# Gate and up products of a gated MLP in the order 1, 7, 6, 2, 5, 3, 4, with their partial sums gathered in two PSUM banks

## The chip, the cores and the metric

The kernel runs on one core of a Trainium2 chip. The metric is the device time of one execution in microseconds (us). The engines are named as the profile names them: PE (TensorE, matrix products into PSUM), PEld (its weight loads), DVE (VectorE), ACT (ScalarE), POOL (GpSimd) and SP (SyncE, which here only issues DMAs). Each engine takes its instructions in the order in which the program lists them; an instruction whose semaphore is not there yet holds up all that stand behind it on the same engine.

## The reference

```python
def _A_ref(x, wqkv, wo):                      # linear attention, 32 heads of 18
    ...
    num = jnp.einsum("bhqd,bhde->bhqe", pq, kv)
    den = jnp.einsum("bhqd,bhd->bhq", pq, z)[..., None] + 1e-6
    o = num / den
    return ... @ wo

def _B_ref(x, w_gate, w_up, w_down):          # gated MLP, 576 -> 4608 -> 576
    g = jnp.einsum("bsd,df->bsf", x, w_gate)
    u = jnp.einsum("bsd,df->bsf", x, w_up)
    h = _gelu(g) * u
    return jnp.einsum("bsf,fd->bsd", h, w_down)

x = A_x                                        # 1 x 2048 x 576, float32
g = _sigmoid((x * gate_w).sum(-1, keepdims=True))
return g * _A_ref(x, ...) + (1 - g) * _B_ref(x, ...)
```

The change concerns the two products with `w_gate` and `w_up` in the second function.

## The kernel before, in words

The program has two parts. The first, some 300 us, projects keys, values and queries and forms the attention half, which goes to DRAM. The second is the MLP. It is a loop over n from 0 to 35 (lines 939 to 1033): 18 slices of 256 hidden columns for the first 1024 tokens (n below 18) and the same 18 slices for the second 1024 tokens. Each pass n has a **gate half** (m = 0) and an **up half** (m = 1).

In a half, the product of the inputs (two feature halves by two groups of 512 tokens) with the slice of weights (two feature halves by two groups of 128 columns) is a 2 by 2 block product. It is done with seven products instead of eight, from sums of the blocks of x (S1 to S4) and of the weights (T1 to T4); `PRODUCTS` (line 36) says which pair each of the seven numbers stands for. Float32 is kept by splitting every operand into a high and a low part, so one of the seven products is 7 matmuls of 512 columns into one PSUM bank (`product`, line 682). The four outputs are P1+P2; P1+P6+P7-P4; P1+P6+P5+P7; P1+P6+P5+P3. `gu_steps` (line 722) lists the seven steps of a half in the order 1, 6, 2, 7, 5, 4, 3. Each step issues one product and then the work of DVE and ACT that takes it out of its bank: step 1 copies P1 to `p1` with ACT (line 765), steps 6, 7, 5, 4 and 3 each add their bank to a running sum in SBUF on DVE (lines 770, 785, 790, 799, 816), and product 2 is added on top of product 1 in the same bank. Product 3 is added on top of product 5, once DVE has read product 5 there. In the gate half a GELU on ACT follows for each of the four outputs (`gelu`, and line 776 straight from PSUM); in the up half DVE multiplies the outputs with the gate (`up`, line 727), and `high` (ACT, line 730) and `low` (DVE, line 733) split the result `es` into `hs`. A half uses five of four rotating banks (`mlp.banks(4)`).

The down product of pass n-1 is spread between the steps of pass n by `next_down`. For n-1 below 18 and for the last pass it comes in 8 tiles of 12 matmuls (`down`, line 839). For n-1 from 18 to 34 (`BLOCKS`) it is a seven-product form too, 14 **units** of 6 matmuls (`unit`, line 870), each of which DVE adds into `sums` (line 881). Units and tiles use two PSUM pairs in turn. After a step i of the gate half two units follow from i = 2 on (in the last pass three from i = 3 on), and one tile from i = 3 on in the other passes; in the up half one follows each of the steps 0 to 3. Where n is 18 or 36, four (then all) tiles come first. So pass 0 has no down work between its steps, and the up halves of n = 18 and n = 35 have none either.

For the units, the rows of `h` must be summed as well: `h_sums` (line 743) has POOL add the four `es` in place, and in steps 0, 1 and 2 of the next pass (`late`) ACT takes the high parts and POOL the low parts (`h_parts`, line 739). The last of these high parts is the one of S4 (step 2), which waits for a sum on POOL that stands behind all the others there. The weights of the units are split by `d_split` (ACT line 678, POOL line 680) once the last unit of the pass before has read the old ones. In the first 18 passes POOL and ACT also split the gate and up weights (`w_sums`, `w_split`), which later passes load back from DRAM. In the last pass POOL combines the seven sums (`combine`, line 890), and DVE adds the attention half (`gated`, line 904).

## Time and profile before

| | us |
|---|---|
| runs | 1557.53, 1553.53, 1555.42; median 1555.42 |
| span of the profiled execution | 1554.6 |
| DVE busy | 989.5 |
| ACT busy | 548.6 |
| POOL busy | 851.2 |
| steps' copies out of PSUM, ACT L765, 72 of them | 43.0 |
| steps' first adds out of PSUM, DVE L770, 72 of them | 49.4 |
| one pass with units (from 1083.12 to 1116.92 on the chain) | 33.80 |

The span runs from the first to the last instruction of one execution. The profiled execution's own time outside its span is not given; its span stands 0.8 us below the median of the runs. A line such as `L690 PE MATMUL bank<-xo,wu` names the line of the program, the engine, the operation, the tile written and the tiles read; `x7` is how many instructions are merged in the row. In a timeline the first number is the start in us from the beginning of the span and the second the time until the end of the last merged instruction. Matmul ends include about 0.2 us of pipeline, so lengths of products are best taken from one start to the next.

### The profile page before, as it was taken

Reading aid. Unit: us, or ns where it says so; the run is one execution under the profiler, and the core shown is the slowest. Engines: PE = TensorE matmul, PEld = TensorE weight load, DVE = VectorE, ACT = ScalarE, POOL = GpSimd, SP = SyncE. Lnnn points to the kernel's source line nnn. Section 1 sums busy time; section 2 is a strip of 40 time slices with the busy share of each in tenths; the row PEclk is TensorE's granted clock in tenths of the full one; section 3 lists DMA queues with packets and bytes.
Section 4 is the critical chain, followed back from the end, with each engine's and each line's share of the span. In section 5 each row is a group of like instructions: output and inputs, shape, how many; then the busy total and the mean of one; then the engine's idle time right before and its main releaser. Section 6 shows DMA issues by size and latency. Waiting matters only on the chain.

```text
span 1554.6 us, 21238 instructions
## 1 busy us (share of the span) xinstructions
PE 1535.8 (99%) x8447; PEld 1358.3 (87%) x8447; DVE 989.5 (64%) x1342; ACT 548.6 (35%) x848; POOL 851.2 (55%) x693
## 2 busy tenths in 40 slices
PE   8999999999999999999999999999999999999997
PEld 8999788888888888888888888888888888888886
DVE  6443767366655555565655556777777767777777
ACT  6544554333433333333333322223232223222221
POOL 1410112276777768686666646556666555666663
PEclk9999999999999999999999999999999999999999
DMA  5611434765556565565545575433443443344333
GB/s 202 194 56 32 154 126 170 254 254 188 204 203 235 218 230 202 188 242 186 215 177 194 202 312 184 180 142 134 175 167 134 148 179 134 141 186 150 134 149 107
DMA packets 53883, 275.26 MB, mean 177 GB/s; under 512 B 4368, under 2 KB 23464, under 8 KB 43160
## 3 DMA queue, kind: packets, MB, share of 16 engines
q1 hardware_dynamic: 49464, 257.26, 44.5%
q10 hardware_dynamic: 2592, 9.31, 1.6%
q0 software_dynamic: 1728, 7.34, 1.2%
q8 instruction: 66, 1.08, 0.3%
q14 instruction: 33, 0.27, 0.1%
HBM read 172.41 MB, written 101.47 MB: 176 GB/s over the span
## 4 chain that ended last, share of the span: by engine, by line
PE 91%; DVE 4%; DMA 2%; issue 1%; ACT 1%; POOL 1%; SPq 0%; ACTq 0%; DVEq 0%; POOLq 0%
PE bank L690 50%; PE pair L852 15%; PE pair L876 12%; PE bank L168 7%; PE bank L333 3%; PE pair L524 2%; PE pair L219 1%; DVE h L733 1%; DMA xc<-xs 1%; DMA wg<-wp_d 1%; POOL xo L476 1%; DVE e L727 0%; DVE sums L904 0%; PE pair L168 0%; PE den L428 0%
## 5 line engine op out<-in xcount | busy, mean ns | idle before, releaser
L690 PE MATMUL bank<-xo,wu 128*128 128x512 f32 x1764 | 435.8, 394 | 5.7 <-DVE p L790 5.7
L690 PE MATMUL bank<-xo,wg 128*128 128x512 f32 x1764 | 433.7, 393 | 0.2 <-DMA wg<-wp_d 0.2
L690 PEld LDWEIGHTS bank<-xo,wu 128*128 128x128 f32 x1764 | 323.4, 188 | 66.7 <-DVE p L790 6.6
L690 PEld LDWEIGHTS bank<-xo,wg 128*128 128x128 f32 x1764 | 324.8, 188 | 64.7 <-DMA wg<-wp_d 0.6
L852 PEld LDWEIGHTS pair<-wd,h 128*128 128x128 f32 x1716 | 243.6, 189 | 13.8 <-DVE wd L67 0.7
L852 PE MATMUL pair<-wd,h 128*128 128x288 f32 x1716 | 250.6, 294 | 0.7 <-DVE wd L67 0.5
L730 ACT ACTIVATE h<-e 128x512 fp32r<-128x512 f32 x127 | 80.4, 633 | 376.3 <-DVE e L727 349.6
L859 DVE SCALAR_TENSOR_TENSOR acc<-pair,gate,acc 128x576 f32<-128x576 f32 x143 | 116.6, 816 | 131.1 <-PE pair L852 131.1
L881 DVE TENSOR_TENSOR sums<-pair,sums 128x576 f32<-128x576 f32 x224 | 167.7, 754 | 34.3 <-PE pair L876 26.5
L733 DVE TENSOR_TENSOR h<-e,h 128x512 fp32r<-128x512 f32 x127 | 131.4, 1035 | 44.8 <-ACT h L730 44.7
L760 ACT ACTIVATE e<-e 128x512 f32<-128x512 f32 x108 | 68.1, 631 | 226.1 <-DVE e L816 93.4
L680 POOL TENSOR_TENSOR wdb<-draw,wdb 128x432 fp32r<-128x432 f32 x34 | 38.4, 1153 | 195.9 <-ACT wdb L678 195.9
L876 PEld LDWEIGHTS pair<-wdb,h 128*128 128x128 f32 x816 | 117.9, 189 | 8.3 <-DVE sums L881 0.6
L876 PE MATMUL pair<-wdb,h 128*128 128x288 f32 x816 | 123.0, 296 | 0.1
L168 PE MATMUL bank<-kvw,xo 128*128 128x378 f32 (+5 forms) x560 | 106.9, 345 | 5.4 <-ACT kvw L66 5.2
L168 PEld LDWEIGHTS bank<-kvw,xo 128*128 128x128 f32 (+1 forms) x560 | 97.0, 192 | 9.9 <-ACT kvw L66 5.6
L618 POOL TENSOR_TENSOR wu<-wuraw,wu 128x768 fp32r<-128x768 f32 x18 | 36.5, 2028 | 119.6 <-ACT wu L617 119.6
L876 PEld LDWEIGHTS pair<-wdb,hx 128*128 128x128 f32 x612 | 89.0, 189 | 6.2 <-DVE sums L881 0.6
L876 PE MATMUL pair<-wdb,hx 128*128 128x288 f32 x612 | 93.0, 296 | 0.1
L765 ACT ACTIVATE p<-bank 128x512 f32<-128x512 f32 x72 | 43.0, 598 | 122.0 <-PE bank L690 121.6
L770 DVE TENSOR_TENSOR u<-bank,p 128x512 f32<-128x512 f32 x72 | 49.4, 686 | 45.0 <-PE bank L690 39.9
L727 DVE TENSOR_TENSOR e<-u,e 128x512 f32<-128x512 f32 x72 | 69.4, 965 | 2.5
(171 smaller groups left out, 2079.2 us busy)
## 6 DMA issues: line engine op xcount, KB each, us to landing
wp_d<-wg SPq DMA_DIRECT2D x17, 2240.0 KB, 6.7
wp_d<-wu SPq DMA_DIRECT2D x17, 2240.0 KB, 8.2
wg<-wp_d SPq DMA_DIRECT2D x17, 2240.0 KB, 8.7
wu<-wp_d SPq DMA_DIRECT2D x17, 2240.0 KB, 8.4
draw<-wdn SPq DMA_DIRECT2D x36, 576.0 KB, 9.4
wgraw<-wgu SPq DMA_DIRECT2D x18, 768.0 KB, 4.4
wuraw<-wgu SPq DMA_DIRECT2D x18, 768.0 KB, 4.5
xo<-xop_d SPq DMA_DIRECT2D x7, 1280.0 KB, 8.1
```

Of the source, the lines that this page charges most:

```text
L168: nc.tensor.matmul(out_t[:, :n], xa, kvw[i][:rows, r, lo:lo + n], start=(k == 0), stop=(k == 13))
L333: nc.tensor.matmul(ps[:R], qw[i][:rows, rw, GO[g]:GO[g] + R], xa, start=(k == 0), stop=(k == 13))
L690: nc.tensor.matmul(ps, w_, x_, start=start and i == 0, stop=i == 6, skip_group_check=not start)
L727: nc.vector.tensor_tensor(es[i], v, es[i], OP.mult)
L730: nc.scalar.activation(hs[i][:, 0], es[i], AF.Copy)
L733: nc.vector.tensor_tensor(hs[i][:, 1], es[i], f32(hs[i][:, 0]), OP.subtract)
L760: nc.scalar.activation(es[i], es[i], AF.Gelu_apprx_tanh)
L770: nc.vector.tensor_tensor(u2, b, p1, OP.add)
L852: nc.tensor.matmul(y[i], h[:, a, c], wd[:, (1 - i, 2 + i)[f], wl], start=(k == 0), stop=(k == 5))
L859: nc.vector.scalar_tensor_tensor(o, v, gate[:, 1, st:st + 1], o, op0=OP.mult, op1=OP.add)
L876: nc.tensor.matmul(y[:, j, :288], h[:, hl, c], wd[:, b, wl], start=(i == 0), stop=(i == 2))
L881: nc.vector.tensor_tensor(o, y[:, :, :288], o, OP.add)
```

## The change

The seven products of a half run in the order 1, 7, 6, 2, 5, 3, 4. Products 1, 6, 5 and 3 are added up in one bank; after 1, 6 and 5 ACT copies the sum so far to `p1`, `u2` and `u3` (`keep_copy`). Products 7 and 4 are added up in a second bank, from which DVE forms two outputs; for this, T4 has its sign turned (`b21 - t2`). Product 2 has a bank of its own, and DVE adds `p1` to it. Three of four banks are taken in a half. The down work of the up half follows steps 1 to 4 instead of 0 to 3, `d_prep` of a last pass moves from step 3 to 4, and `h_sums` and all its parts are queued behind the last step. The four banks of the MLP are opened before the first step instead of after the attention part is done.

```diff
-SEQUENCE = (1, 6, 2, 7, 5, 4, 3)
+SEQUENCE = (1, 7, 6, 2, 5, 3, 4)
...
+        def keep_copy(dst, src):
+            nc.scalar.activation(dst, src, AF.Copy)
         def s1():
             ps["a"] = bank()
             product(1, m, ps["a"], True)
-            nc.scalar.activation(p1, ps["a"], AF.Copy)
+            keep_copy(p1, ps["a"])
+        def s7():
+            ps["b"] = bank()
+            product(7, m, ps["b"], True)
         def s6():
-            b = bank()
-            product(6, m, b, True)
-            nc.vector.tensor_tensor(u2, b, p1, OP.add)
+            product(6, m, ps["a"], False)
+            keep_copy(u2, ps["a"])
         def s2():
-            a = ps["a"]
-            product(2, m, a, False)
+            c = bank()
+            product(2, m, c, True)
+            nc.vector.tensor_tensor(es[0] if m == 0 else p1, c, p1, OP.add)
             if m == 0:
-                nc.scalar.activation(es[0], a, AF.Gelu_apprx_tanh)
+                gelu(0)
             else:
-                up(0, a)
+                up(0, p1)
                 high(0)
                 low(0)
...
         def s5():
-            d = ps["d"] = bank()
-            product(5, m, d, True)
-            nc.vector.tensor_tensor(es[3] if m == 0 else p1, d, u3, OP.add)
+            product(5, m, ps["a"], False)
+            keep_copy(u3, ps["a"])
+            nc.vector.tensor_tensor(es[3] if m == 0 else u3, ps["b"], u3, OP.add)
             if m == 0:
                 gelu(3)
             else:
-                up(3, p1)
+                up(3, u3)
+        def s3():
+            product(3, m, ps["a"], False)
+            if m == 0:
+                nc.scalar.activation(es[1], ps["a"], AF.Gelu_apprx_tanh)
+            else:
+                up(1, ps["a"])
+                high(3)
+                low(3)
         def s4():
-            e = bank()
-            product(4, m, e, True)
-            nc.vector.tensor_tensor(es[2] if m == 0 else u3, u3, e, OP.subtract)
+            product(4, m, ps["b"], False)
+            nc.vector.tensor_tensor(es[2] if m == 0 else u2, ps["b"], u2, OP.add)
...
+                up(2, u2)
                 if blocks:
-                    late[1] = h_sums()
...
+                    then = h_sums()
+                    late[0] = lambda i: (i == 0 and (high(1), low(1)), then(i))
+                else:
+                    high(1)
+                    low(1)
+                    if seam:
+                        high(2)
+                        low(2)
+                    else:
+                        late[0] = lambda i: i == 0 and (high(2), low(2))
-        return [s1, s6, s2, s7, s5, s4, s3]
+        return [s1, s7, s6, s2, s5, s3, s4]
...
-            if i < 4:
+            if 0 < i < 5:
                 next_down()
-            if i == 3 and final:
+            if i == 4 and final:
                 d_prep(last)
             if blocks and i == 4:
                 d_split()
```

How the rows move, at three places. First ACT in a gate half with units (n from 19 to 35). `h`, `hx` are the parts of S3, S1, S2 and S4, `e` the four outputs, `p`, `u` the kept sums; what a row waits for stands in brackets. Before, from the first copy of the half to its last GELU:

```order
L765 ACTIVATE p1_2551<-bank_8551 128x512 [waits PE_49,Activation_49]
L730 ACTIVATE h0_2916<-e0_2554 128x512 [waits DVE_49]
L678 ACTIVATE wdb_8033<-draw2_8034 128x3x288 [waits DMAHW0_49,PE_49]
L678 ACTIVATE wdb_8033<-dsum_8035 128x4x288 [waits Pool_49]
L730 ACTIVATE h3_2919<-e3_2915 128x512 [waits DVE_49]
L765 ACTIVATE p1_2551<-bank_8665 128x512 [waits PE_49]
L730 ACTIVATE h1_2917<-e1_2913 128x512 [waits DVE_49,Activation_49]
L740 ACTIVATE hx1_8038<-sx_8036 128x512 [waits Activation_49,Pool_49]
L740 ACTIVATE h2_2918<-e2_2914 128x512 [waits Activation_49,Pool_49]
L740 ACTIVATE hx0_8037<-e3_2915 128x512 [waits Activation_49]
```

And now, from the same copy to the copy of `u3`:

```order
L731 ACTIVATE h0_2916<-e0_2554 128x512 [waits DVE_49]
L764 ACTIVATE u3_2553<-bank_8202 128x512 [waits PE_49,Activation_49]
L679 ACTIVATE wdb_7959<-draw2_7960 128x3x288 [waits DMAHW5_49,PE_49]
L679 ACTIVATE wdb_7959<-dsum_7961 128x4x288 [waits Pool_49]
L731 ACTIVATE h3_2919<-e3_2915 128x512 [waits DVE_49]
L764 ACTIVATE p1_2551<-bank_8314 128x512 [waits PE_49]
L731 ACTIVATE h1_2917<-e1_2913 128x512 [waits DVE_49]
L741 ACTIVATE hx1_7964<-sx_7962 128x512 [waits Pool_49]
L741 ACTIVATE h2_2918<-e2_2914 128x512 [waits Pool_49]
L741 ACTIVATE hx0_7963<-e3_2915 128x512
```

The row `hx_8039<-e` of before (now `hx_7965<-e`) is the high part of S4. Behind it stood GELUs of a finished output; now the copy of P1+P6+P5 to `u3` stands behind it and behind the first GELU.

Second, PE in the same gate half, from the fifth product on. `bank` rows are products, `pair` rows are units. Before, product 5, two units and product 4:

```order
L690 MATMUL bank_8745<-xo_130,wg_2445 128x512 x7
L876 MATMUL pair_8755<-wdb_8033,hx1_8038 128x288 [waits DVE_49,Activation_49]
L876 MATMUL pair_8755<-wdb_8033,hx1_8038 128x288
L876 MATMUL pair_8755<-wdb_8033,hx1_8038 128x288 [waits Pool_49]
L876 MATMUL pair_8755<-wdb_8033,hx1_8038 128x288 x3
L876 MATMUL pair_8763<-wdb_8033,hx1_8038 128x288 [waits DVE_49]
L876 MATMUL pair_8763<-wdb_8033,hx1_8038 128x288 x5
L690 MATMUL bank_8771<-xo_130,wg_2445 128x512 x7
```

Now product 5, two units and product 3:

```order
L691 MATMUL bank_8581<-xo_130,wg_2445 128x512 [waits Activation_49]
L691 MATMUL bank_8581<-xo_130,wg_2445 128x512 x6
L874 MATMUL pair_8671<-wdb_7959,hx1_7964 128x288 [waits DVE_49]
L874 MATMUL pair_8671<-wdb_7959,hx1_7964 128x288
L874 MATMUL pair_8671<-wdb_7959,hx1_7964 128x288 [waits Pool_49]
L874 MATMUL pair_8671<-wdb_7959,hx1_7964 128x288 x3
L874 MATMUL pair_8679<-wdb_7959,hx1_7964 128x288 [waits DVE_49]
L874 MATMUL pair_8679<-wdb_7959,hx1_7964 128x288 x5
L691 MATMUL bank_8581<-xo_130,wg_2445 128x512 [waits Activation_49]
L691 MATMUL bank_8581<-xo_130,wg_2445 128x512 x6
```

Before, neither product waited here. Now both are added to the same bank, and each waits for the ACT copy that reads it (of `u2` and `u3`).

Third, PE at the end of an up half, where the units are `pair` rows. Before, product 7, the last unit, and products 5, 4 and 3:

```order
L690 MATMUL bank_8608<-xo_130,wu_2446 128x512 x7
L876 MATMUL pair_8617<-wdb_8033,hx2_8039 128x288 [waits DVE_49]
L876 MATMUL pair_8617<-wdb_8033,hx2_8039 128x288 x5
L690 MATMUL bank_8625<-xo_130,wu_2446 128x512 x7
L690 MATMUL bank_8641<-xo_130,wu_2446 128x512 x7
L690 MATMUL bank_8625<-xo_130,wu_2446 128x512 [waits DVE_49]
L690 MATMUL bank_8625<-xo_130,wu_2446 128x512 x6
```

And now, from product 5:

```order
L691 MATMUL bank_8469<-xo_130,wu_2446 128x512 [waits Activation_49]
L691 MATMUL bank_8469<-xo_130,wu_2446 128x512 x6
L874 MATMUL pair_8545<-wdb_7959,hx2_7965 128x288 [waits DVE_49]
L874 MATMUL pair_8545<-wdb_7959,hx2_7965 128x288 x5
L691 MATMUL bank_8469<-xo_130,wu_2446 128x512 [waits Activation_49]
L691 MATMUL bank_8469<-xo_130,wu_2446 128x512 x6
L691 MATMUL bank_8479<-xo_130,wu_2446 128x512 [waits DVE_49]
L691 MATMUL bank_8479<-xo_130,wu_2446 128x512 x6
```

The last unit of the up half, which is the last that reads the old down weights, stood ahead of the last three products; now it stands ahead of the last two.

More of the change, by code (lines that the diff above doesn't have):

```diff
@@ L273, in make @@
             t1, t2, t3, t4 = (self.sums[:, i] for i in range(4))
-            for o, a, b in ((t1, b12, b11), (t2, b22, t1), (t3, b22, b12), (t4, t2, b21)):
+            for o, a, b in ((t1, b12, b11), (t2, b22, t1), (t3, b22, b12), (t4, b21, t2)):
                 nc.gpsimd.tensor_tensor(o, a, b, OP.subtract)
@@ L316, in tile_gated_mix @@
     mixing = Scope()
-    mixing.banks(3)
-    denp = mixing.stack.enter_context(tc.tile_pool(name="denp", bufs=1, space=PSUM, reuse_waits="tile"))
+    mixps = Scope()
+    mixps.banks(3)
+    denp = mixps.stack.enter_context(tc.tile_pool(name="denp", bufs=1, space=PSUM, reuse_waits="tile"))
     rp = mixing.pool("rp", bufs=3)
@@ L610, in w_sums @@
         t1, t2, t3, t4 = (tsum[:, i] for i in range(4))
-        for o, a, b in ((t1, b12, b11), (t2, b22, t1), (t3, b22, b12), (t4, t2, b21)):
+        for o, a, b in ((t1, b12, b11), (t2, b22, t1), (t3, b22, b12), (t4, b21, t2)):
             nc.gpsimd.tensor_tensor(o, a, b, OP.subtract)
@@ L764, in s1 @@
             product(1, m, ps["a"], True)
-            nc.scalar.activation(p1, ps["a"], AF.Copy)
+            keep_copy(p1, ps["a"])
+        def s7():
+            ps["b"] = bank()
+            product(7, m, ps["b"], True)
         def s6():
-            b = bank()
-            product(6, m, b, True)
-            nc.vector.tensor_tensor(u2, b, p1, OP.add)
+            product(6, m, ps["a"], False)
+            keep_copy(u2, ps["a"])
         def s2():
-            a = ps["a"]
-            product(2, m, a, False)
+            c = bank()
+            product(2, m, c, True)
+            nc.vector.tensor_tensor(es[0] if m == 0 else p1, c, p1, OP.add)
             if m == 0:
-                nc.scalar.activation(es[0], a, AF.Gelu_apprx_tanh)
+                gelu(0)
             else:
-                up(0, a)
+                up(0, p1)
                 high(0)
                 low(0)
-        def s7():
-            c = bank()
-            product(7, m, c, True)
-            nc.vector.tensor_tensor(u3, c, u2, OP.add)
         def s5():
-            d = ps["d"] = bank()
-            product(5, m, d, True)
-            nc.vector.tensor_tensor(es[3] if m == 0 else p1, d, u3, OP.add)
+            product(5, m, ps["a"], False)
+            keep_copy(u3, ps["a"])
+            nc.vector.tensor_tensor(es[3] if m == 0 else u3, ps["b"], u3, OP.add)
             if m == 0:
@@ L802, in s4 @@
             else:
-                up(2, u3)
-                high(3)
-                low(3)
+                up(2, u2)
                 if blocks:
-                    late[1] = h_sums()
-        def s3():
-            d = ps["d"]
-            if m == 1 and not blocks:
-                high(2)
-                if seam:
-                    low(2)
-            product(3, m, d, False)
-            nc.vector.tensor_tensor(es[1] if m == 0 else u2, d, u2, OP.add)
-            if m == 0:
-                gelu(1)
-            else:
-                up(1, u2)
-                if seam:
+                    then = h_sums()
+                    late[0] = lambda i: (i == 0 and (high(1), low(1)), then(i))
+                else:
                     high(1)
                     low(1)
-                elif blocks:
-                    late[0] = lambda i: i == 0 and (high(1), low(1))
-                else:
-                    late[0] = lambda i: i == 0 and (high(1), low(2), low(1))
-        return [s1, s6, s2, s7, s5, s4, s3]
+                    if seam:
[4 more added lines that the diff above has]
+        return [s1, s7, s6, s2, s5, s3, s4]
     def acc_load(p, t):
@@ L905, in gated @@
                                        mix_of(t).rearrange("p (n c) -> p n c", n=2), op0=OP.mult, op1=OP.add)
+    mixps.close()
+    mlp.banks(4)
     first_steps = gu_steps(0)
@@ L920, in tile_gated_mix @@
     mixing.close()
-    mlp.banks(4)
     hp0 = mlp.pool("hp0")
```

## The prediction

> **What bounds the kernel now.** I read the page's busy times first.
>
> ```profile
> span 1554.6 us, 21238 instructions
> ...
> PE 1535.8 (99%) x8447; PEld 1358.3 (87%) x8447; DVE 989.5 (64%) x1342; ACT 548.6 (35%) x848; POOL 851.2 (55%) x693
> ...
> L881 DVE TENSOR_TENSOR sums<-pair,sums 128x576 f32<-128x576 f32 x224 | 167.7, 754 | 34.3 <-PE pair L876 26.5
> ```
>
> PE is the bound: it is idle for 18.8 us in all. The change adds no matmul and takes none away, so it can win only from those 18.8 us, and it loses whatever new waits PE gets. The list of waits, PE alone, shows how little is to be won:
>
> ```profile
> PE bank L690 <- DVE p L790: 5.7, 2, 5.2
> ...
> PE bank L690 <- DMA wg<-wp_d: 0.2, 1, 0.2
> ```
>
> The first row is product 3 waiting for DVE to read product 5 out of the same bank: twice, once for 5.2 us (in the last pass). Between them stands nothing over 0.7 us in the MLP. So the question is whether the new waits for ACT are as well hidden as the old ones for DVE. I therefore took one pass with units from the timeline, engine by engine. PE, from the first product of a gate half (1087.78):
>
> ```profile
> 1087.78 5.00 PE L690 MATMUL bank<-xo,wg 128*128 128x512 f32 x21
> 1092.62 1.77 PE L876 MATMUL pair<-wdb,h 128*128 128x288 f32 x12
> 1094.23 1.79 PE L690 MATMUL bank<-xo,wg 128*128 128x512 f32 x7
> 1095.85 1.75 PE L876 MATMUL pair<-wdb,h 128*128 128x288 f32 x12
> ```
>
> Start to start, three products take 4.84 us (1.61 each), two units 1.60 (0.80 each). ACT and POOL in the same stretch:
>
> ```profile
> 1083.16 0.93 ACT L678 ACTIVATE wdb<-draw 128x864 fp32r<-128x864 f32 x1 [1.86 <-PE pair L876]
> ...
> 1089.60 0.60 ACT L765 ACTIVATE p<-bank 128x512 f32<-128x512 f32 x1 [2.01 <-PE bank L690]
> ...
> 1096.48 0.58 ACT L776 ACTIVATE e<-bank 128x512 f32<-128x512 f32 x1
> 1100.45 0.63 ACT L740 ACTIVATE hx<-e 128x512 fp32r<-128x512 f32 x1 [3.39 <-POOL e L737]
> 1100.98 0.62 ACT L760 ACTIVATE e<-e 128x512 f32<-128x512 f32 x1
> ```
>
> ```profile
> 1084.17 2.21 POOL L680 TENSOR_TENSOR wdb<-draw,wdb 128x432 fp32r<-128x432 f32 x2 [12.34 <-ACT wdb L678]
> 1086.33 3.73 POOL L680 TENSOR_TENSOR wdb<-dsum,wdb 128x576 fp32r<-128x576 f32 x2
> 1090.68 1.29 POOL L737 TENSOR_TENSOR e<-e,e 128x512 f32<-128x512 f32 x1 [0.63 <-DVE h L733]
> ...
> 1099.12 1.29 POOL L737 TENSOR_TENSOR e<-e,sx 128x512 f32<-128x512 f32 x1
> ```
>
> The reader is to see the row at 1100.45: ACT stands idle for 3.39 us until POOL's seventh instruction, counted from 1090.68, is through (1099.12 + 1.29 = 1100.41), and only then takes the high part of S4. Today this harms nobody: behind it is a GELU that PE does not wait for.
>
> **The change, part by part.**
>
> *The new wait in gate halves with units (n = 19 to 34, 16 passes).* In the ACT rows of the change, the copy to `u3` is third after this S4 part (S4, first GELU, `u3`), and product 3 cannot start before it. Without waits PE would run products 1, 7, 6 from 1087.78, two units from 1092.62, product 2 from 1094.22, two units, product 5 from 1097.43, two units from 1099.04 and product 3 from 1100.64. When is `u3` there? POOL's work is first moved later. The down weights are split once the last unit has read the old ones; that unit now stands one product (1.61) later, so ACT L678 starts at 1084.77, POOL's run over `wdb`, which ended at 1090.06, ends at 1091.67, and the sum that began at 1090.68 begins then, 0.99 later. From that sum to the S4 part on ACT the rows give 1100.45 - 1090.68 = 9.77, so S4 is taken at 1101.44. Back to back, ACT's starts lie 0.53 apart (1100.45 to 1100.98): GELU at 1101.97, `u3` at 1102.50, and with 0.60 for a copy out of a bank and 0.05 for the handover PE goes on at 1103.15. That is a wait of 1103.15 - 1100.64 = **2.5 us per pass**, 16 x 2.5 = 40.0. A part of it already falls on product 5, which waits for `u2` behind the parts of S3 and S1; the end is the same.
>
> Bounds for it: if S4 comes no later than today (1100.45), the wait is 1.5; if DVE never gets in POOL's way, the four splits take 2.21 + 2.75 (two of 576 columns, row at 1527.43 below) and end at 1090.74, and seven sums and parts of 1.29 end at 1099.8, which leaves 0.85. If DVE gets in the way once more (0.7, one of its instructions), 3.2. I take 2.5, the value with the contention that the rows show.
>
> *Pass 35, gate half.* Three units stand between products 5 and 3 and there are two pairs. The third unit needs the first one's pair, whose DVE add is queued behind the add that waits for `u3`: 1103.10 + 0.69 + 0.75 (L881's mean, 754 ns) and handovers make 1104.65. Its turn would be at 1087.78 + 4.84 + 1.60 + 1.61 + 2.40 + 1.61 + 1.60 = 1101.44. **3.2 us.** Queued behind the same add in the other passes are the sums of two units; the next unit wants its pair only after product 3, when they are done.
>
> *The other `u3` waits.* From the start of the next slot, ACT begins 0.20 after a product (1089.60 against 1087.78 + 1.61), copies 0.60 and hands over: 0.85. One unit (0.80) covers nearly all of it in up halves: 16 x 0.05 = 0.8. A tile or two units cover it in the other gate halves and in passes 1 to 17: 0. In pass 0 nothing covers it: 0.85 in its gate half. In the up halves of passes 0 and 18 nothing covers it either, and ACT first has the high part of the first output, which waits for two DVE instructions: from the end of product 2, 0.20 + 0.69 + 0.69 + 0.63 + 0.60 with handovers make 2.9, product 5 covers 1.61: 1.3 each. In pass 18 this hides the 0.2 that PE now waits for weights. Sum 0.8 + 0.85 + 1.3 + 1.1 = **4.0 us**.
>
> *The seam after pass 17.* The down product that follows at once uses outputs 3 and 2 first. Output 2 is now the last one made. The timeline of before:
>
> ```profile
> 914.25 1.88 PE L690 MATMUL bank<-xo,wu 128*128 128x512 f32 x7 [0.53 <-DVE p L790]
> ...
> 916.90 2.91 PE L852 MATMUL pair<-wd,h 128*128 128x288 f32 x20 [0.24 <-DVE h L733]
> ```
>
> These two waits (0.8) go. After the last product DVE still has a low part (until 1.0), then an add, the multiplication and two low parts of 0.7 each: 3.8. The first tile's last two matmuls (0.27) start then instead of ending with the tile at 1.6: 2.5 lost, 0.8 won: **+1.7**.
>
> *The last pass's up half.* Here is the old 5.2.
>
> ```profile
> 1507.98 19.48 POOL L890 TENSOR_TENSOR sums<-sums 128x576 f32<-128x576 f32 x14
> 1527.43 2.75 POOL L668 TENSOR_TENSOR wdb<-draw,wdb 128x576 fp32r<-128x576 f32 x2
> ```
>
> ```profile
> 1523.59 7.13 DVE L733 TENSOR_TENSOR h<-e,h 128x512 fp32r<-128x512 f32 x1 [0.70 <-ACT h L730]
> ...
> 1531.43 0.69 DVE L790 TENSOR_TENSOR p<-bank,u 128x512 f32<-128x512 f32 x1
> 1532.15 0.69 DVE L727 TENSOR_TENSOR e<-p,e 128x512 f32<-128x512 f32 x1
> ...
> 1532.17 3.35 PE L690 MATMUL bank<-xo,wu 128*128 128x512 f32 x7 [5.18 <-DVE p L790]
> 1532.76 0.81 DVE L904 SCALAR_TENSOR_TENSOR sums<-sums,gate,dsum 128x576 f32<-128x576 f32 x1
> ```
>
> A DVE instruction with both inputs in SBUF, 0.7 us elsewhere, took 7.13 because POOL's run of sixteen went through without a gap; all behind it were late. In the change, the first such instruction is the multiplication behind product 2, and the high part on ACT waits for it, `u3` behind that, product 3 behind that. Counted from the first product of this half (1517.16 before): POOL's fourteen end at 10.3 (the last two now come after, since the split they wait for moves behind product 5), multiplication to 11.05, high part, copy, product 3 at 12.3 instead of 8.05, product 4 to 15.5. DVE then still has ten instructions of 0.7 to 0.8 and one or two waits for ACT and POOL, and frees the first tile at about 20.9; two tiles end at 22.5. Before, they ended at 1539.34, which is 22.2. Term **+0.5**, between -3 (if DVE slips in earlier) and +5. The Trainium skill ("SBUF — State Buffer", section "Who interferes with whom") says that whichever of DVE and GpSimd issues first holds the shared port for that one instruction. By it DVE would wait 1.4 us at most and the term would be about 1.6 lower, the sum 1603. The row of 7.13 speaks against it here, so the trace's value stays.
>
> *What is removed.* Two of five DVE adds per half go (144 x 0.69 = 99 us), and two ACT copies come (144 x 0.60, less 36 GELUs that now read SBUF instead of a bank, at the same 0.6). PE waits for neither outside the places above, so both count nothing. Earlier banks before pass 0: the queries' banks are free by then, nothing.
>
> **Sum**: 40.0 + 3.2 + 4.0 + 1.7 + 0.5 = 49.4. On the span it gives 1604.0; the profiled span is 0.8 below the median of the runs, and 1555.4 + 49.4 = **1605**.
>
> **Rivals.**
> - *The S4 part comes in time* (not slower). ACT is busy a third of the time, and today PE never waits for a copy of it. Decided by S4's start: up to 1098.9 the wait is nothing (1100.64 less 1.71 for the rest of the chain). Then the small terms remain, 4.0 + 1.7 with +0.5 to -3 for the end: 1558 to 1562, the middle 1560; under 1551 only if the whole 5.2 at the end and the slow clock behind it were won and the small terms hidden too. Against it: POOL's row at 1099.12 alone ends after 1098.9, already before its shift.
> - *POOL runs freely*: waits of 0.85 and the small terms, 16 x 0.85 + 1.5 + 5 = 20, 1575. For it: DVE has 99 of its 989.5 us less to do. Against it: the instructions of DVE that collided with the splits remain.
> - *The clock falls in each wait.* After product 5 of the last pass PE stood still, and the granted clock (third column from the end of these windows) halved 3.4 us later:
>
> ```profile
> 1527.00:1530.30 3.30, 0.00 (x0) 0.00 (x0) 3.30 (x1) 0.00 (x0) 3.18 (x3) 1.00 0.69 216
> 1530.40:1537.00 6.60, 4.83 (x14) 4.15 (x15) 6.43 (x11) 1.26 (x2) 0.00 (x0) 0.50 0.00 1
> ```
>
> The half clock lasted 6.6 us, so each fall costs about 3.3: 17 x 3.3 = 56, 1661. It decides from a standstill of 3.4 us; mine is 2.5, in two pieces. The Trainium skill ("TensorE: Matmul & The Clock Gate", section "A second HAM failure mode: psum-queue depth-cycling") reports that even short, frequent idle times between bursts on cycling banks make the clock swing. By that page the time would be 1661; no row here shows it for gaps below a microsecond.
> - That the change doesn't do what it says is excluded by the rows: the copies stand there and PE waits for them.
>
> **Chances.** Forecast 0.74; POOL free 0.10; clock 0.06; S4 in time 0.10 (of it 0.03 faster, 0.06 the same, 0.01 slower). Low end: waits of 0.85 with the small terms and -3 at the end, 13.6 + 1.5 + 4.0 with 1.7 - 3, about +16 to 1571. High end: 16 x 3.2 + 4.2 + 5 + 2.5 + 5 = 68, 1624. Range 1570 to 1626; clock and "in time" are left out. A measurement of this kernel tells 0.3% (4.7 us) from no change: faster 0.03, same 0.06, slower 0.91.
>
> **What would show it.** In the list of waits, PE bank <- ACT `u` should lead with some 40 us in about 17 long and 17 or more short waits; a pass with units should take 36.3 instead of 33.8 us; ACT's S4 part should start 13.7 us after the first product of the gate half, and passes 1 to 17 should stay at their length. It is wrong if the S4 part comes before 11 us, if passes without units grow, or if the granted clock falls below 1 between 955 and 1500 us.

## The result, and the profile after

The changed kernel takes 1613.83 us (median of four runs, 1613.62 to 1614.31), the kernel before 1555.54 us in runs beside them (1553.53 to 1557.53): ratio 1.0372, 95% interval 1.0358 to 1.0387. It is slower by 58.3 us; the prediction had said 49.4.

The page of the changed kernel: span, busy times, and the groups of the products and of the new copies (busy us and mean ns, then the idle time ahead of the group and what ended it).

```profile
span 1612.2 us, 21093 instructions
...
PE 1552.9 (96%) x8447; PEld 1362.7 (85%) x8447; DVE 882.4 (55%) x1198; ACT 627.6 (39%) x992; POOL 854.0 (53%) x693
...
L691 PE MATMUL bank<-xo,wg 128*128 128x512 f32 x1764 | 439.3, 396 | 33.8 <-ACT u L764 33.7
L691 PE MATMUL bank<-xo,wu 128*128 128x512 f32 x1764 | 437.5, 395 | 5.0 <-ACT u L764 5.0
...
L764 ACT ACTIVATE u<-bank 128x512 f32<-128x512 f32 x144 | 85.0, 590 | 134.1 <-PE bank L691 134.1
```

And its list of PE's waits (us in total, times, longest):

```profile
PE bank L691 <- ACT u L764: 38.7, 41, 2.4
...
PE pair L874 <- DVE sums L879: 2.1, 1, 2.1
```

DVE has 107 us less to do than before, and the kernel is slower all the same: PE now idles for 59.3 us instead of 18.8, nearly all of the difference ahead of products that wait for a copy (L764) which takes ACT only 0.59. The reader is to see the releaser and the group together: a short instruction, with ACT busy 39% of the time, and 41 waits for it. It must have been late in starting, which the ACT rows below show. The span grew by 57.6 us, of which 40.5 are this idle time; the other 17.1 stand in PE's busy time (1552.9 against 1535.8). Modelled ends reach some 0.2 us into each wait, the products behind a wait take a little longer (see the end), and three stretches at half clock lengthen their matmuls.

Starts of the gate halves in the two traces give the length of each pass, and so where the time went. Up to the start of the last matmul the differences come to 57.7 us (the rest is rounding):

| stretch | before, us | after, us | difference | forecast |
|---|---|---|---|---|
| until pass 0 | 270.45 | 271.76 | +1.3 | 0 |
| pass 0 | 43.36 | 48.69 | +5.3 | +2.2 |
| pass 1 | 36.14 | 35.32 | -0.8 | 0 |
| passes 3, 5, ... 13, each | 35.33 | 36.02 to 36.09 | +4.3 in all | 0 |
| pass 17 (seam) | 42.99 | 44.63 | +1.6 | +1.7 |
| pass 18 | 29.45 | 30.91 | +1.5 | +1.1 |
| passes 20 to 34, each | 33.80 | 36.46 | +41.9 with pass 19 | +40.8 |
| pass 35 | 55.94 | 58.47 | +2.5 | +3.7 |

The first line is open: in the experiments that build on the changed kernel pass 0 starts between 270.7 and 272.0, in the one that builds on the kernel before (e4) at 269.8. The spread within one kind is as large as the difference, but the two kinds don't overlap, so a part of it may belong to the change. Pass 1 is shorter since the kernel before waits 0.5 there for down weights and the change, whose pass 0 is longer, does not.

Now one gate half with units, the same as in the prediction (pass 23), from the timeline of the changed kernel. PE:

```profile
1111.03 5.00 PE L691 MATMUL bank<-xo,wg 128*128 128x512 f32 x21
1115.87 1.77 PE L874 MATMUL pair<-wdb,h 128*128 128x288 f32 x12
1117.47 1.79 PE L691 MATMUL bank<-xo,wg 128*128 128x512 f32 x7
1119.10 1.75 PE L874 MATMUL pair<-wdb,h 128*128 128x288 f32 x12
1121.26 1.88 PE L691 MATMUL bank<-xo,wg 128*128 128x512 f32 x7 [0.41 <-ACT u L764]
1122.98 1.76 PE L874 MATMUL pair<-wdb,hx 128*128 128x288 f32 x12
1126.26 1.89 PE L691 MATMUL bank<-xo,wg 128*128 128x512 f32 x7 [1.51 <-ACT u L764]
```

ACT, and of POOL the beginning of its split of the down weights and the seventh of its instructions on `h`:

```profile
1107.03 0.60 ACT L764 ACTIVATE u<-bank 128x512 f32<-128x512 f32 x1 [0.31 <-PE bank L691]
1107.78 0.93 ACT L679 ACTIVATE wdb<-draw 128x864 fp32r<-128x864 f32 x1
...
1124.57 0.63 ACT L741 ACTIVATE hx<-e 128x512 fp32r<-128x512 f32 x1 [3.37 <-POOL e L738]
1125.11 0.61 ACT L761 ACTIVATE e<-e 128x512 f32<-128x512 f32 x1
1125.62 0.58 ACT L764 ACTIVATE u<-bank 128x512 f32<-128x512 f32 x1
```

```profile
1108.78 2.73 POOL L681 TENSOR_TENSOR wdb<-draw,wdb 128x432 fp32r<-128x432 f32 x2 [15.52 <-ACT wdb L679]
...
1123.25 1.28 POOL L738 TENSOR_TENSOR e<-e,sx 128x512 f32<-128x512 f32 x1
```

Without waits product 3 would start 12.87 after the first product. It starts at 1126.26, which is 15.23. Product 5 ended long before, near 1123. ACT stood idle for 3.37 us ahead of the row at 1124.57, the part of S4; only when POOL had made its sum (1123.25 + 1.28) did ACT go on to a GELU and then to the copy at 1125.62. The copy's own data had been there since product 5.

### The profile page after: what moved, and what is told of

It reads as the page before. It is cut to its first block, busy times and chain, and to the rows that moved or that the text cites. A ratio compares the mean times of both kernels' runs of the same rounds, so it can differ in the third digit from the quotient of the medians.

```text
span 1612.2 us, 21093 instructions
## 1 busy us (share of the span) xinstructions
PE 1552.9 (96%) x8447; PEld 1362.7 (85%) x8447; DVE 882.4 (55%) x1198; ACT 627.6 (39%) x992; POOL 854.0 (53%) x693
## 4 chain that ended last, share of the span: by engine, by line
PE 67%; POOL 15%; DVE 7%; ACT 6%; issue 4%; DMA 1%; SPq 0%; ACTq 0%; DVEq 0%; POOLq 0%
PE bank L691 34%; PE pair L850 12%; PE bank L168 7%; PE pair L874 7%; POOL wdb L681 5%; POOL e L738 4%; POOL hx L742 3%; PE bank L334 3%; PE pair L525 2%; DVE e L728 2%; POOL sx L738 1%; PE pair L219 1%; ACT wdb L679 1%; DVE h L734 1%; ACT wu L618 1%
## 5 line engine op out<-in xcount | busy, mean ns | idle before, releaser
L691 PE MATMUL bank<-xo,wg 128*128 128x512 f32 x1764 | 439.3, 396 | 33.8 <-ACT u L764 33.7
L681 POOL TENSOR_TENSOR wdb<-draw,wdb 128x432 fp32r<-128x432 f32 x34 | 46.3, 1383 | 249.0 <-ACT wdb L679 249.0
L734 DVE TENSOR_TENSOR h<-e,h 128x512 fp32r<-128x512 f32 x127 | 124.8, 983 | 36.0 <-ACT h L731 33.8
L764 ACT ACTIVATE u<-bank 128x512 f32<-128x512 f32 x144 | 85.0, 590 | 134.1 <-PE bank L691 134.1
L874 PEld LDWEIGHTS pair<-wdb,h 128*128 128x128 f32 x816 | 118.3, 189 | 9.6 <-DVE sums L879 2.6
L874 PE MATMUL pair<-wdb,h 128*128 128x288 f32 x816 | 123.3, 296 | 2.1 <-DVE sums L879 2.1
L764 ACT ACTIVATE p<-bank 128x512 f32<-128x512 f32 x72 | 43.2, 599 | 140.5 <-PE bank L691 140.1
L874 PEld LDWEIGHTS pair<-wdb,hx 128*128 128x128 f32 x612 | 89.5, 190 | 6.6 <-POOL hx L742 0.8
L874 PE MATMUL pair<-wdb,hx 128*128 128x288 f32 x612 | 93.3, 297 | 0.6 <-POOL hx L742 0.5
L793 DVE TENSOR_TENSOR e<-bank,u 128x512 f32<-128x512 f32 x36 | 24.9, 692 | 114.9 <-ACT u L764 114.9
```

The source lines that it names most:

```text
L681: nc.gpsimd.tensor_tensor(wd[:, i, 1, c], src[:, :, c], f32(wd[:, i, 0, c]), OP.subtract)
L691: nc.tensor.matmul(ps, w_, x_, start=start and i == 0, stop=i == 6, skip_group_check=not start)
L734: nc.vector.tensor_tensor(hs[i][:, 1], es[i], f32(hs[i][:, 0]), OP.subtract)
L764: nc.scalar.activation(dst, src, AF.Copy)
L874: nc.tensor.matmul(y[:, j, :288], h[:, hl, c], wd[:, b, wl], start=(i == 0), stop=(i == 2))
```

## The experiments

Ten kernels were run, each beside the kernel before on the same chip. Two theories stood against each other at first. **Queue**: the copies are late because ACT takes its instructions in order and stands at parts that wait for POOL. **Copy**: a copy out of a bank ahead of every further product is itself too long for the cover it has. The first experiments undo or move one thing each; the later ones take away, one by one, the waits that were left.

### e1: parts behind the copies

```diff
                 if i == 0:
                     h_parts(S2, sx)
-                elif i == 1:
+                elif i == 2:
                     h_parts(S3, es[2])
                     h_parts(S1, es[3])
-                elif i == 2:
                     h_sum(es[1], es[1], sx, OP.subtract)
+                elif i == 4:
                     h_parts(S4, es[1])
```

> Changed kernel, but ACT takes the parts of S3 and S1 behind the copy to u2, and the part of S4 behind the copy to u3; POOL's order is kept. Queue theory (PE waits because the copies stand behind ACT instructions that wait for POOL): the gate-half waits of 0.57 and 1.67 us go, passes 20 to 34 fall from 36.46 us to 33.9 to 34.2, pass 35 loses some 4 us, whole time 1566 to 1577 us. Rival, POOL itself is too late for PE: PE then waits for POOL's low parts, passes stay above 35.5, whole time above 1600. Rival, reading a bank between two products that are added up there costs PE by itself: passes stay at 36.4, 1612.

Measured: 1569.45 us, ratio 1.0081 (1.0051 to 1.0110); 44.4 us of the loss are gone. ACT in the same gate half, which here starts at 1098.90:

```profile
1106.22 0.63 ACT L741 ACTIVATE hx<-sx 128x512 fp32r<-128x512 f32 x1 [4.39 <-POOL sx L738]
1106.76 0.58 ACT L764 ACTIVATE u<-bank 128x512 f32<-128x512 f32 x1
...
1110.38 0.60 ACT L764 ACTIVATE u<-bank 128x512 f32<-128x512 f32 x1 [1.23 <-PE bank L691]
...
1112.49 0.62 ACT L741 ACTIVATE hx<-e 128x512 fp32r<-128x512 f32 x1
```

The copy at 1110.38 now waits for PE, not PE for it, and product 3 starts at 1111.78, 12.88 after the first product. The same number of copies, of the same length, costs these gate halves nothing: the queue it was. What is left per pass is 0.13 (33.93), in the up half. Pass 35 came 2.5 us down where some 4 had been expected.

### e2: the copies on DVE

```diff
-            keep_copy(u2, ps["a"])
+            nc.vector.tensor_copy(u2, ps["a"])
...
-            keep_copy(u3, ps["a"])
+            nc.vector.tensor_copy(u3, ps["a"])
```

> Changed kernel, with u2 and u3 copied by DVE instead of ACT; S parts stay where they are. Queue theory: ACT may wait for POOL as long as it likes, passes 20 to 34 at 33.9 to 34.3 us, whole time 1566 to 1580 us. Rival, reading the bank between two products costs by itself: passes stay near 36.4, 1612. Rival, DVE's own queue is as late as ACT's: PE waits for DVE, passes in between, 1585 to 1600.

Measured: 1604.47 us, ratio 1.0306 (1.0276 to 1.0335): a miss, above the range of the rival that named DVE's queue. The gate halves are as they should be, with product 3 at 12.87, but PE now waits 36 times for DVE, 37.0 us in all. DVE and PE in the up half of a pass with units:

```profile
1148.97 0.69 DVE L734 TENSOR_TENSOR h<-e,h 128x512 fp32r<-128x512 f32 x1 [0.70 <-ACT h L731]
1149.58 0.75 DVE L879 TENSOR_TENSOR sums<-pair,sums 128x576 f32<-128x576 f32 x1
1150.25 0.68 DVE L792 COPY u<-bank 128x512 f32<-128x512 f32 x1
```

```profile
1150.99 2.35 PE L691 MATMUL bank<-xo,wu 128*128 128x512 f32 x9 [1.03 <-DVE u L792]
```

It is the same fault on another engine. DVE's copy of `u3` stands behind the low part of the first output (L734), which waits for ACT's high part, and behind a unit's add. Which engine copies matters less than what stands ahead of the copy.

### e3 and e4: the units' place in the up half

The prediction put POOL's later start (0.99 us) down to the last unit, which now stands one product later. e3 is the change with the units back after steps 0 to 3; e4 is the kernel before with its units moved to steps 1 to 4.

```diff
-            if 0 < i < 5:
+            if (i < 4 if n - 1 in BLOCKS else 0 < i < 5):
```

> Changed kernel, with the units of the up half after steps 0 to 3 as in the kernel before (so the split of the down weights starts one product earlier). If the moved unit makes POOL late and POOL sets the S4 part: the S4 part on ACT comes about 1 us earlier, the gate-half waits fall from 2.25 to about 1.2 us, while in the up half u3 is no longer covered and costs 0.9 to 1.4 us; passes 36.0 to 36.8 us, whole time 1607 to 1618 us. If the unit's place does not matter for POOL: gate-half waits stay and the up half's come on top, passes 37.5 us, whole time 1630 us.

```diff
-            if i < 4:
+            if (0 < i < 5 if n - 1 in BLOCKS and not last else i < 4):
```

> Kernel before with one part of the change alone: the units of the up half after steps 1 to 4, so that the split of the down weights and POOL's sums start later. Queue theory: nothing that PE waits for stands behind the S4 part there, passes stay at 33.8 us, whole time 1554 to 1558 us. Rival, late POOL by itself holds PE up: passes above 34.5 us, whole time above 1566 us.

Measured: e3 1620.94 us, ratio 1.0411 (1.0381 to 1.0442); e4 1556.26 us, ratio 0.9999 (0.9987 to 1.0010), its passes 33.76. e3 lies between its two forecasts. From e4, a later POOL harms nobody where no copy stands behind its results. In e3, where the gate half starts at 1112.28, ACT shows:

```profile
1108.26 0.60 ACT L764 ACTIVATE u<-bank 128x512 f32<-128x512 f32 x1 [0.31 <-PE bank L691]
1108.76 0.92 ACT L679 ACTIVATE wdb<-draw 128x864 fp32r<-128x864 f32 x1
...
1125.45 0.63 ACT L741 ACTIVATE hx<-e 128x512 fp32r<-128x512 f32 x1 [3.36 <-POOL e L738]
```

ACT's half of the split (L679) starts 3.52 ahead of the gate half; in the change it was 3.25, in the kernel before 4.62. With the units back in their old place most of the delay is still there. It is ACT's queue once more: the split stands behind the copy of `u3` at 1108.26, which waits for product 5. But e4, where the units are late and no such copy exists, has the delay too. ACT there, in a gate half that starts at 1086.64:

```profile
1083.63 0.93 ACT L678 ACTIVATE wdb<-draw 128x864 fp32r<-128x864 f32 x1 [4.26 <-PE pair L876]
...
1100.24 0.64 ACT L740 ACTIVATE hx<-e 128x512 fp32r<-128x512 f32 x1 [3.38 <-POOL e L737]
```

Its split starts 3.01 ahead of the gate half, 1.61 later than before, and its S4 part comes at 13.60 (before 12.67, in the change 13.54). So each of the two alone delays the split, the units' place by 1.61 and the copy by 1.10, and together they don't add up. Taking the units back brought little, because the copy stood there as well: in e3 the S4 part comes at 13.17, product 3 at 14.86 instead of 15.23. The up half, in turn, loses a unit's cover and waits 0.75 for `u3`, so the kernel is slower than the change.

### e5 and e6: first output's high part, and preparation of the inputs

e5 is e1 with the high and low part of an up half's first output taken behind the copy of `u3`. e6 is e5 with the conversion of the inputs' sums (`sums_ahead`, n from 2 to 13) moved from step 0 to step 3.

```diff
                 up(0, p1)
-                high(0)
-                low(0)
...
             keep_copy(u3, ps["a"])
+            if m == 1:
+                high(0)
             nc.vector.tensor_tensor(es[3] if m == 0 else u3, ps["b"], u3, OP.add)
...
                 up(3, u3)
+                low(0)
```

> e1_parts_behind, and in the up half the high part of the first output stands on ACT behind the copy to u3 instead of ahead of it. Queue theory: in the up halves of passes 0 and 18, where no unit covers it, the wait for u3 falls from 2.5 and 1.7 us to 0.85; in pass 0 the half clock after the long wait (1.4 us) goes too. Pass 0 at 44 to 44.6 us (47.2 in e1), pass 18 at 29.8 to 30.1 (30.7), whole time 1564 to 1567.5 us. Rival, what holds u3 up there is something else (POOL's port, the bank): passes 0 and 18 and the whole time as in e1, 1569.

```diff
-                if 2 <= n < 14:
-                    sums_ahead(n // 2 - 1, n % 2)
+            if i == 3 and 2 <= n < 14:
+                sums_ahead(n // 2 - 1, n % 2)
```

> e5_high0_behind, and the ACT conversion of the second group's input sums (odd passes 3 to 13) moves from step 0 to step 3, behind the copy to u2. Queue theory: the wait of 0.7 us for u2 in these six passes goes, they fall from 36.05 to 35.35 us, whole time 4.2 us below e5. Rival, that wait comes from the split of the up weights on ACT alone: nothing changes, or the wait moves to u3.

Measured: e5 1571.07 us, ratio 1.0098 (1.0077 to 1.0119), a miss; e6 1566.79 us, ratio 1.0063 (1.0045 to 1.0081).

e5 shortens pass 0 as far as the wait goes: 45.35 us instead of 47.17. The 44 to 44.6 that were expected had also counted on a half clock that e1's pass 0, its base, did not have (see the rivals below). In the change, DVE and ACT in the up half of pass 0 had read:

```profile
312.42 1.93 DVE L728 TENSOR_TENSOR e<-p,e 128x512 f32<-128x512 f32 x1
...
314.38 0.63 ACT L731 ACTIVATE h<-e 128x512 fp32r<-128x512 f32 x1 [3.84 <-DVE e L728]
314.92 0.58 ACT L764 ACTIVATE u<-bank 128x512 f32<-128x512 f32 x1
...
315.55 5.06 PE L691 MATMUL bank<-xo,wu 128*128 128x512 f32 x14 [2.35 <-ACT u L764]
```

A multiplication that takes 0.69 elsewhere takes 1.93 while POOL's splits run, and high part, copy and product follow behind it. With the high part moved, PE's wait falls from 2.35 to 0.75. But e5 gave the gain back at the seam after pass 17 (47.35 us, against 44.64 in e1) and in pass 35 (57.93 against 56.00). In pass 35 PE's wait for `u3` falls from 2.87 to 0.69, but PE then waits 2.32 for POOL's down weights, and the clock is halved for 6.83 us instead of 3.41. PE at the seam of e5:

```profile
923.51 0.53 PE L851 MATMUL pair<-wd,h 128*128 128x288 f32 x2 [0.67 <-DVE h L734]
925.50 4.69 PE L851 MATMUL pair<-wd,h 128*128 128x288 f32 x18 [1.46 <-ACT h L731]
```

And of the change, with the same two waits (of 0.66 and 1.46 in e1 too):

```profile
926.74 0.53 PE L850 MATMUL pair<-wd,h 128*128 128x288 f32 x2 [0.66 <-DVE h L734]
928.73 2.84 PE L850 MATMUL pair<-wd,h 128*128 128x288 f32 x18 [1.46 <-ACT h L731]
```

Eighteen matmuls take 4.69 us in one and 2.84 in the other. The windows behind the waits give the granted clock (third from the end), of e5 and then of the change:

```profile
926.00:932.00 6.00, 6.00 (x28) 6.00 (x28) 1.81 (x3) 0.00 (x0) 0.00 (x0) 0.53 0.79 327
```

```profile
929.00:936.00 7.00, 7.00 (x48) 6.55 (x48) 3.80 (x6) 0.00 (x0) 0.00 (x0) 1.00 0.94 385
```

So this part of the miss is not a queue: the clock fell at a place where it had not fallen before, after equal waits. What it lost at the seam is therefore no property of the edit.

e6 met its expectation. The six odd passes had each lost 0.7; the change's ACT rows in pass 3 were:

```profile
396.85 1.47 ACT L618 ACTIVATE wu<-tsum 128x1536 fp32r<-128x1536 f32 x1
398.23 1.04 ACT L706 ACTIVATE xuh<-xu 128x1024 fp32r<-128x1024 f32 x1
399.17 0.57 ACT L764 ACTIVATE u<-bank 128x512 f32<-128x512 f32 x1
```

A conversion of 1.04 us stood ahead of the copy of `u2`. In e6 it stands behind:

```profile
393.13 1.47 ACT L618 ACTIVATE wu<-tsum 128x1536 fp32r<-128x1536 f32 x1
394.50 0.58 ACT L764 ACTIVATE u<-bank 128x512 f32<-128x512 f32 x1
...
395.50 1.05 ACT L706 ACTIVATE xuh<-xu 128x1024 fp32r<-128x1024 f32 x1
```

The odd passes are back at 35.32, the 4.2 us that were expected.

### e7 to e10: the rest of the waits

e7 is e6 with, in up halves, two units behind product 5 and none behind product 7, the parts of the third output ahead of the second's where a down product follows at once, and two of the last pass's additions of the attention half (`gated`) behind its last step. e8 is e7 with another order of tiles at the seam after pass 17, the second output split first. e9 is e8 with the last pass's split of down weights (`d_prep`) three steps earlier. e10 is e8 with product 3 in a bank of its own, added by DVE, in the four halves that have no down work.

```diff
-                next_down()
+                if n - 1 not in BLOCKS:
+                    next_down()
+                elif i > 1:
+                    next_down(2 if i == 4 else 1)
...
-            if last and i in (4, 5):
-                gated(i)
+            if last and i == 6:
+                gated(4)
+                gated(5)
```

> e6_inputs_later, and three more: in the up half two units behind step 5 (none behind step 1), the low part of output 2 ahead of that of output 1 where a down product follows at once, and the last pass's first two DVE mixes behind its last step. Queue theory: passes 20 to 34 at 33.75 to 33.8 us (-2.1 in all), pass 17 some 0.7 us and pass 35 1 to 3 us shorter, whole time 1554 to 1559 us, the same as the kernel before within 0.3%. Rival, fewer DVE adds are worth time once no copy is late: below 1551 us. Rival, the split of the down weights, 0.8 us later, delays the first units: passes above 34.2, 1563 or more.

```diff
-                high(3)
-                low(3)
+                k = 1 if seam and not last else 3
+                high(k)
+                low(k)
...
-            downs = deque((lambda t=t: down(n - 1, t)) for t in ([4, 5, 6, 7, 0, 1, 2, 3] if seam else range(8)))
+            downs = deque((lambda t=t: down(n - 1, t)) for t in ([4, 5, 6, 7, 0, 1, 2, 3] if n == NQD else range(8)))
```

> e7_all, and at the seam after pass 17 the down tiles that read outputs 0 and 1 come first, with output 1 split before outputs 3 and 2. Theory (the seam waits for the output that is made last, and the half clock there follows from these waits): the 1.6 us of waits and the 2.7 us of half clock go, pass 17 from 47.4 to 43.0 us, whole time 1553.5 to 1556 us, 0 to 0.3% under the kernel before. Rival, the half clock there has another cause: pass 17 stays above 45.5 us, 1557 us.

```diff
-            if i == 4 and final:
+            if i == (1 if last else 4) and final:
```

> e8_seam, and in the last pass the split of the down weights on ACT comes behind step 1 of the up half instead of step 4, so POOL can go straight on to the low parts. Theory: the 2.2 us that PE waits for POOL's low parts before the last tiles go, but POOL's port is taken without a gap while DVE needs it, as in the kernel before; pass 35 between 1 us longer and 2.5 us shorter than in e8, whole time 1551 to 1556 us.

```diff
-            product(3, m, ps["a"], False)
+            v = ps["a"]
+            if bare():
+                d = bank()
+                product(3, m, d, True)
+                v = es[1] if m == 0 else u3
+                nc.vector.tensor_tensor(v, d, u3, OP.add)
+            else:
+                product(3, m, v, False)
```

> e8_seam, and in the four halves without down work between their steps (both of pass 0, the up halves of passes 18 and 35) product 3 gets a bank of its own and a DVE add, so it no longer waits for the copy to u3. Theory (each such wait costs 0.85 us and about 0.1 at the restart): pass 0 from 45.5 to 43.5 to 43.8 us, pass 18 from 30.1 to 29.2, pass 35 up to 0.9 shorter, whole time 1553.5 to 1556 us, some 3 us under e8 and 0 to 0.2% under the kernel before. Rival, the wait only moves to the next product or to the first down tiles: whole time as e8, 1558 us.

| kernel | median, us | ratio to before (95%) | passes 20 to 34 | pass 0 | pass 17 | pass 35 |
|---|---|---|---|---|---|---|
| before | 1556.4 to 1557.0 | 1 | 33.80 | 43.36 | 42.99 | 55.94 |
| e7 | 1558.92 | 1.0014 (1.0004 to 1.0023) | 33.77 | 45.55 | 47.40 | 54.26 |
| e8 | 1558.09 | 1.0013 (1.0004 to 1.0022) | 33.77 | 45.53 | 44.46 | 53.22 |
| e9 | 1559.87 | 1.0023 (1.0012 to 1.0033) | 33.77 | 45.51 | 44.46 | 55.75 |
| e10 | 1559.88 | 1.0024 (1.0015 to 1.0033) | 33.77 | 44.22 | 44.44 | 56.71 |

e7 is within its expectation, 0.14% above the kernel before, though pass 17 did not get shorter as expected; its seam ran at half clock as in e5 and e6. DVE is busy for 870.6 us in it and PE waits in no pass from 20 to 34. The DVE adds that the change takes away thus have their test here: with the new waits gone and 119 us less of DVE's work, a pass is 0.03 us shorter than before, and e4 has 33.76 with all of DVE's adds in place. e8 mends the seam, from 47.40 to 44.46, and missed its expected total by 2 us; pass 17 was expected at 43.0, but a wait of 1.3 us for DVE's accumulation and one of 0.5 for ACT stayed. e9 missed too: its pass 35 is 2.5 us longer than e8's, where 1 had been the most. PE's wait for POOL in the last pass went, as it should, but DVE's multiplication behind product 2 shows what came instead:

```profile
1528.92 5.20 DVE L728 TENSOR_TENSOR e<-p,e 128x512 f32<-128x512 f32 x1
```

```profile
1514.16 16.67 POOL L891 TENSOR_TENSOR sums<-sums 128x576 f32<-128x576 f32 x12
1530.78 2.79 POOL L669 TENSOR_TENSOR wdb<-draw,wdb 128x576 fp32r<-128x576 f32 x2
```

POOL now goes from its sums straight on to the two splits and leaves no gap until 1533.57; the multiplication ends at 1534.12. In e8, where the splits came later, it took 2.49. It is the stretched instruction of the prediction (7.13 there), now on the path to product 4, which waits 2.50 us for it, and the clock halves behind that wait. e10 went as its rival had it: pass 0 is shorter by 1.3 and pass 18 by 1.0, but pass 1 is longer by 1.6 (its first tile now waits 0.9 for the down weights), pass 19 by 0.9, and pass 35 by 3.5, with half clock in it.

No version beat the kernel before.

## Why the prediction was right, and where not

**The mechanism and its main term were right.** The forecast was 2.5 us per gate half with units, out of the S4 part at 13.66 after the first product and the copy at 14.72. Measured: 13.54, 14.59, and product 3 at 15.23, 2.36 late; the gate half is 21.77 us long instead of 19.30, +2.47. e1 moved nothing but the parts' places in the queues of ACT and POOL and brought the gate half back to 19.30. The whole came out some 8 us above the forecast, nearly all of it from two terms: pass 0 (3.1) and the odd passes (4.3), which had been put at nothing.

**The up halves with units were mis-sized**: 0.05 forecast, 0.19 measured, 3 us over 16 passes in place of 0.8. The term counted the wait that a unit does not cover and left out that a product which had to wait takes longer from its start to the next: 1.72 instead of 1.62 (1121.26 to 1122.98 above, 1117.47 to 1119.10 without a wait).

**Why POOL was late was right, but not the whole.** The forecast was 0.99 for the last unit's later place; the S4 part came 0.87 later, and e4, with that place alone, shows 0.93. But e3 shows a second reason that would have been enough for 0.50: ACT's split of the down weights stands behind the copy of `u3`. The prediction had applied the rule on what stands behind a waiting instruction to PE's products alone, and not to the split behind the same kind of copy in the half before. It cost the forecast nothing, since the two don't add up, but whoever had put only the units back, as e3 does, would have won 0.37 of the 0.87.

**Pass 0 was mis-sized**: 0.85 + 1.3 against 5.3. The chain through the high part was the right one, and e5 confirms it; but the multiplication in it was put at 0.69 and took 1.93 beside POOL, and the half clock came on top. The prediction had counted the port for the last pass and forgotten POOL's splits in pass 0.

**"Passes 1 to 17 should stay at their length" was wrong** for the odd passes from 3 to 13, +4.3; growth of passes without units was one of the prediction's own signs of being wrong. The tile that was to cover the copy of `u3` does so; the copy of `u2` stood behind a conversion of 1.04 us, which e6 showed by moving it.

**The seam** (+1.7 forecast, +1.64 measured) and pass 18 (+1.1, +1.46) were right.

**The last pass** came to +2.5 instead of +3.7. Its gate half lost 4.06, not 3.2: the third unit waited for DVE's add behind the add that waits for `u3`, as said (L874 <- DVE `sums`, 2.1), and the clock halved behind it. Its rest won 1.5 instead of losing 0.5, half clock from 1593.49 on included: DVE's multiplication came at 1583.83, when POOL's run had just ended (1583.45), so nothing held it. That run ended 7.06 after the half's first product, not 10.3 as forecast. In e1, whose gate half there is 3.0 us shorter, it ended 9.34 after it and PE waited 2.87 for `u3`. So the loss ahead paid for a part of the gain, and that the two came out near the forecast together is in part luck. The range given there (-3 to +5) had this case as its lower side. The Trainium skill ("SBUF — State Buffer", section "Who interferes with whom") has the loser of the shared port blocked for the length of one instruction. Of this, 1.93 in pass 0 would fit; 5.20 in e9 beside a run of POOL instructions without a gap (1.39 each) does not, so the trace's value was the right choice.

**The rivals.** "S4 in time" and "POOL runs freely" fall with the row at 1124.57. "The clock falls in each wait" did not happen in the sixteen passes; the window from 955 to 1500 us shows it at full:

```profile
955.00:1500.00 545.00, 515.03 (x2708) 443.10 (x2707) 314.06 (x401) 177.28 (x285) 304.17 (x244) 1.00 0.39 146
```

But its deciding point, a standstill of 3.4 us, was wrong. In pass 0 the clock fell behind the wait of 2.35, in pass 35 behind that of 2.1 (windows of the changed kernel, the clock third from the end):

```profile
317.00:320.20 3.20, 3.20 (x9) 2.42 (x9) 2.47 (x3) 1.26 (x2) 3.20 (x3) 0.50 1.05 442
...
1566.30:1569.40 3.10, 3.10 (x10) 2.45 (x9) 0.76 (x1) 0.01 (x1) 3.10 (x3) 0.50 0.00 0
```

In e1 the same wait in pass 0, also 2.35, left the clock full. This explains the 1.5 us between pass 0 of the two (48.69 and 47.17). What decided can be read from the traces. The half clock begins in the change at 316.90, 1566.18 and 1593.49, which lie 366 and 8 times 3.413 us apart: the clock is set anew on a fixed grid of such steps. In the change 2.06 of the 2.35 fall into the step that ends at 316.90; in e1 a border of its grid, at 313.69, cuts the wait in two. The step of the change, and then the two of e1 (behind the length, PE's busy time and the number of matmuls):

```profile
313.49:316.90 3.41, 1.35 (x6) 1.14 (x7) 2.68 (x4) 1.11 (x2) 3.25 (x3) 1.00 0.63 266
```

```profile
310.28:313.69 3.41, 2.43 (x11) 1.62 (x9) 2.45 (x2) 0.00 (x0) 3.25 (x3) 1.00 0.94 358
313.69:317.10 3.41, 2.04 (x9) 1.70 (x10) 2.65 (x5) 1.23 (x3) 3.25 (x3) 1.00 0.73 307
```

The last section has the count over all traces. By it the waits of 0.41 and 1.51 were safe: wherever the grid had lain, no stretch of 3.413 us in pass 23 has under 3,520 columns of matmuls, and no clock fell behind more than 2,850. Pass 0's single wait was a gamble: about half of the positions of the grid leave a step under 2,850 there (an estimate, from sliding the step over the trace). The prediction had two grounds against this rival, a wait below 3.4 us and its two pieces. The first would not have kept the clock, so 0.06 was too little on that ground; the second did.

**Two slips of the sum** changed nothing: the low end of the range adds up to 17.8 and 1573, not 16 and 1571, and the two ends of the last pass, 22.5 and 22.2, lie 0.3 apart, not 0.5.

## What to carry to other kernels

Where the busiest engine may not go on until another engine has read a bank, list what stands ahead of that read in the other engine's queue, back to the last instruction that waits for a third engine; the read costs what the slowest of these costs, whatever its own length. Put such reads ahead of everything that waits for a slower engine, also work of other stages that happens to share the queue, and look again at what now stands behind the read. Taking work off an engine that nobody waits for brings next to nothing: here 119 us of it were worth at most 0.03 us in a pass with units. And a single wait of 2 us or more of the matmul engine can cost more than itself, by the half clock behind it, and need not do so in another run.

## What the runs showed of the hardware

- **The granted clock is set on a grid of 3.413 us, by how much PE streamed in the step just ended.** In each of the twelve traces all changes of the granted clock lie whole numbers of 3.413 us apart, and the grid lies elsewhere against the kernel in each. Counted were the columns that matmuls streamed in each step (512 for a matmul of a product, 288 for one of a unit or tile, those that a border cuts in part; at most some 7,600). The clock halved at the end of all 18 full-clock steps with up to 2,850 columns, and at the end of none of the some 5,400 others, the least of which had 3,000. Between the first record of full clock, some 10 to 13 us in, and the last matmul there is no exception. Half clock stayed after steps with up to 3,200 columns and went after those with 3,550 or more. The same two waits at the seam left 2,740 columns in one step in e5 and 3,000 in e1; the 2.35 us of pass 0 left 2,780 in the change, and 4,950 and 4,290 in two steps in e1. The least in the sixteen passes of the change was 3,540. The Trainium skill ("TensorE: Matmul & The Clock Gate", section "What's actually happening") speaks of an idle window of about 3.4 us that runs freely, not started by the kernel. The grid agrees with the freely running window; that 2.35 us suffice does not agree with one that must be idle throughout. How the chip itself measures the work isn't shown, only that this count parts the cases.
- **A product that had to wait** takes about 0.10 us longer from its start to that of the next group (1.72 against 1.62), seen after every wait for a copy in the passes with units. The cause wasn't tried.
- **A DVE instruction with two inputs in SBUF** took 0.69 us alone, and 1.93 (pass 0), 2.49 (e8) and 5.20 (e9) in like places while POOL's instructions ran beside it, longest where these left no gap. Why it gets in between them at one place and not at another stays open.
